# Decode attention plus gated MLP on one core: heads taken in pairs, projections and output sums moved to VectorE, and every engine's program made of loops

## The chip, the cores and the metric

The kernel runs on one core of one Trainium2 chip. The metric is the device time of one execution in microseconds (us). Before the change the median of 3 runs is 745.85 us (745.75 to 746.23). A core has five engines with programs of their own: TensorE (PE, its weight loads shown as PEld), VectorE (DVE), ScalarE (ACT), GpSimd (POOL) and SyncE (SP), which here issues nearly all loads. Programs meet only at semaphores.

## The reference

One token x of 576 elements is normalised; the result goes through attention over a cache of 8192 positions with 32 heads of 128, and through a gated MLP of 4608; both outputs are added to x. All is float32.

```
xn = layernorm(x)
q = (xn @ wq), 32 heads of 128
scores = q . k_cache / sqrt(128);  p = softmax(scores);  o = p . v_cache
A = o.reshape(4096) @ wo
h = relu(xn @ W_gate) * (xn @ W_up)
out = x + A + h @ W_down
```

The inputs are 134.2 MB of keys, as much of values, and 50.8 MB of weights: 319.2 MB read once, with two operations or so per element.

## The kernel before, in words

A *tile* is 128 partitions by 16384 floats, 8.389 MB, and SBUF holds three of them (`slots`). For head n the tile `("t", n)` carries the values of head n-1 (tile 0: weights) beside the keys of head n, so that a slot is free when TensorE has used those values (mark `("V", n-4)`) and VectorE those keys (`("mr", n-3)`). SyncE's program (`load`, line 159, called from lines 164 to 181) is one list of loads on one queue, each with its wait: three weight tiles, 32 key-and-value tiles, the last values with gate weights and nine output chunks, then the other output weights in shrinking pieces, then the output.

Before the heads, TensorE multiplies xn with wq, W_gate and W_up in 512-column pieces (lines 222 to 231 and `gates`); q is turned into a column per head (`turn`, `qs`).

Each key tile has 128 partitions with 64 positions each. For each head VectorE multiplies all 64 x 128 elements by the query, which TensorE has spread over all partitions in PSUM (`product`, line 287), sums them to 64 scores a partition (`sums`, line 292) and takes their maximum mr (line 293). TensorE spreads the 128 maxima over the partitions (`maxima`), VectorE reduces them to a common bound nb (`bound`, line 296), ScalarE makes the exponentials (`soft`, line 306), and TensorE multiplies them with the values (`values`), into bank bo. After three heads (G = 3) ScalarE copies bo out (`rows`, line 310), TensorE folds it (`outputs`), and VectorE divides by the sums (`close`, lines 299 and 300). TensorE's ten turns of three heads are a loop (`repeat`, `emit`); the programs of the other engines are written out in full.

At the end TensorE multiplies each of 68 output chunks of 128 x 576 (32 of wo, 36 of W_down) with its column of os or hh, into two banks, which are added (line 412) and copied out (lines 413 and 414).

Of the kernel before, what the change touches and what calls it, by code (L numbers as in the profile page):

```python
# [3 lines left out]
F32 = mybir.dt.float32  # L4
# [3 lines left out]
PE_ENGINE = mybir.EngineType.PE  # L8
# [9 lines left out]
G = 3  # L18
NIT = (H - 2) // G
# [5 lines left out]
OUT = ((9,), (28,), (9, 7, 5, 4, 3), (1, 1, 1))  # L25

LAST = 4

UNITS = (28, 32, 16, 5)


STEP = 16

HEAD = 12


class Program:
# [4 lines left out]

    def __init__(self, nc):
        self.nc = nc
        self.sems = {}
        self.counts = {}
        self.marks = {}
        self.lists = {e: [] for e in ("sync", "scalar", "vector", "gpsimd", "tensor")}
        self.loop = None

    def sem(self, name):
        if name not in self.sems:
            self.sems[name] = self.nc.alloc_semaphore(f"s_{name}")
            self.counts[name] = 0
        return self.sems[name]

    def add(self, engine, f, waits=(), mark=None, on=None, by=1):
        to = None
        if mark is not None:
            to = on or engine  # L60
            self.sem(to)
            self.counts[to] += by
            assert mark not in self.marks, mark
            self.marks[mark] = (to, self.counts[to])
        self.lists[engine].append((f, tuple(waits), to, by))

    def repeat(self, begin, times, renamed):


        self.loop = (begin, len(self.lists["tensor"]), times)  # L70
        base = sum(to is not None for _, _, to, _ in self.lists["tensor"][:begin])
        body = {m: v for m, (to, v) in self.marks.items() if to == "tensor" and v > base}
        for m in body:
            del self.marks[m]
        for k in range(times):
            for m, v in body.items():
                self.marks[renamed(m, k)] = ("tensor", v + k * len(body))
        self.counts["tensor"] += (times - 1) * len(body)

    def emit(self, engine, eng):  # L80
        lines = self.lists[engine]
        if engine == "tensor":
            begin, end, times = self.loop
            self.run(eng, lines[:begin])
            with self.nc.Fori(STEP, STEP * (times + 1), STEP, engines=[PE_ENGINE], head_slot={PE_ENGINE: HEAD}) as i:
                self.run(eng, lines[begin:end], i)
            self.run(eng, lines[end:])
        else:
            self.run(eng, lines)

    def run(self, eng, lines, counter=None):
        for f, waits, to, by in lines:
            need = {}
            for w in waits:
                if w[0] == "round":
                    eng.wait_ge(self.sem(w[1]), counter)
                    continue
                s, v = self.marks[w]
                need[s] = max(need.get(s, 0), v)
            for s, v in need.items():  # L100
                eng.wait_ge(self.sem(s), v)  # L101
            i = f(eng)
            if to is not None:
                i.then_inc(self.sem(to), by)


def build(nc, x, kv, vw, wq, wqt, wg, wod, out):
    pr = Program(nc)
    add = pr.add

# [6 lines left out]
    slots = [sb(f"slot{i}", [P, W]) for i in range(3)]  # L117
    ident = sb("ident", [P, P])
    sel = sb("sel", [P, 4 * G])
    x2 = sb("x2", [P, N2])  # L120
    ones = sb("ones", [P, 1])
    one = ones[:1, :]
    eps = sb("eps", [1, 1])
    sm = sb("sm", [1, 8])
# [5 lines left out]
    xn = pzs[:1, :6 * P]  # L130
    xz = sb("xz", [P, 4, 37])
    xt = sb("xt", [P, 37])
    row = sb("row", [P, 576])
    xr = row[:1, :]
    row = row[:, :512]
    gr = sb("gr", [P, 512])
    qs = sb("qs", [P, H])
    dq = sb("dq", [P, G, P])
    hh = sb("hh", [P, 4, 9])
    os = sb("os", [P, H])  # L140
# [6 lines left out]
    bq, bb, bm, bo, bt, acc, ac2, bx = [bank(f"bank{i}") for i in range(8)]  # L147
    qb = bb[:, :G * DH].rearrange("p (h d) -> p h d", d=DH)
    pm = bm[:, :P]
    px = bm[:, 128:136]  # L150
    ot = bt[:, :G]
    pl = bt[:, 8:8 + G]
    turned = bx.rearrange("p (b n) -> p b n", b=4)
# [3 lines left out]
    def load(name, k, src, waits, on, start=0):  # L157
        dst = slots[k % 3][:, start:start + src.shape[-1]]
        add("sync", lambda e: e.dma_start(dst, src), waits, name, on=on, by=16)  # L159

    def tile(n):
        return slots[(n + 3) % 3]

    load("wq", 0, wq, (), "dwq")
    load("g0", 1, wqt, (), "dg0")
    load("g1", 2, wg, (), "dg1")
    load(("t", 0), 3, kv[0], ("pq",), "dt0")
    load(("t", 1), 4, kv[1], ("u0",), "land0")
    load(("t", 2), 5, kv[2], ("u1",), "land1")
    load(("t", 3), 6, kv[3], ("u2", ("mr", 0)), "land2")  # L170
    for n in range(4, H):
        load(("t", n), n + 3, kv[n], (("V", n - 4), ("mr", n - 3)), f"land{(n - 1) % G}" if n < H - 1 else "dlast")
    load(("t", H), H + 3, vw, (("V", H - 4), ("mr", H - 3)), "dvw")
    f = OUT[0][0]
    for k, loads in enumerate(OUT[1:]):
        free = ((("V", H - 3), ("mr", H - 2)), (("V", H - 2), ("mr", H - 1)), (("V", H - 1), "u3", ("first", OUT[0][0] - 1)))[k]
        i = 0
        for n in loads:
            load(("o", f), H + 4 + k, wod[:, (f - 9) * D:(f - 9 + n) * D], free, f"do{f}", i * D)
            i += n  # L180
            f += n
    add("sync", lambda e: e.dma_start(out, xr), (("end", 0), ("end", 1)), "out", on="dout", by=16)


    add("gpsimd", lambda e: e.memset(ident, 0.0), (), "id0")
    add("gpsimd", lambda e: e.affine_select(out=ident, in_=ident, compare_op=ALU.not_equal, fill=1.0, base=0,
                                            pattern=[[-1, P]], channel_multiplier=1), ("id0",), "ident")
    add("gpsimd", lambda e: e.memset(x2, 0.0), (), "x20")
    add("gpsimd", lambda e: e.memset(xz, 0.0), (), "xz0")
    add("gpsimd", lambda e: e.memset(xt, 0.0), (), "xt0")  # L190
    add("gpsimd", lambda e: e.memset(pzs, 0.0), ("px",), "pz0")


    add("scalar", lambda e: e.dma_start(xr, x), (), "xr", on="dxr", by=16)
    add("scalar", lambda e: e.dma_start(x2[64:P:32, :], x.rearrange("o (j q) -> (o j) q", j=2)), ("x20",), "x2", on="dx2", by=16)
    add("vector", lambda e: e.memset(ones, 1.0))
    add("vector", lambda e: e.memset(eps, EPS))
    add("vector", lambda e: e.memset(xn, 0.0), (), "n0")
    add("vector", lambda e: e.reduce_sum(sm[:, 0:1], xr, axis=AX.X), ("xr",), "n1")
    add("vector", lambda e: e.tensor_scalar_mul(sm[:, 1:2], sm[:, 0:1], 1.0 / D), ("n1",), "n2")  # L200
    add("vector", lambda e: e.tensor_scalar(xr, xr, sm[:, 1:2], None, op0=ALU.subtract), ("n2",), "n3")
    add("scalar", lambda e: e.activation(xn[:, :D], xr, AF.Square, accum_out=sm[:, 2:3]), ("n3",), "n4")
    add("scalar", lambda e: e.activation(sm[:, 3:4], sm[:, 2:3], AF.Sqrt, bias=eps, scale=1.0 / D), ("n4",), "n5")
    add("vector", lambda e: e.reciprocal(sm[:, 4:5], sm[:, 3:4]), ("n5",), "n6")
    add("vector", lambda e: e.tensor_scalar_mul(xn[:, :D], xr, sm[:, 4:5]), ("n6",), "n7")
    add("vector", lambda e: e.tensor_copy(xn[:, 704:768], xn[:, 512:576]), ("n7",), "xn")

    add("vector", lambda e: e.reduce_sum(sel, ident.rearrange("p (j m) -> p m j", j=4)[:, :4 * G, :], axis=AX.X), ("ident",), "sel")
    for name, t in (("bo", bo), ("acc", acc), ("ac2", ac2)):
        add("vector", lambda e, t=t: e.memset(t, 0.0), (), name + "0")  # L210

    add("vector", lambda e: e.tensor_copy(xz[:, :, 5], px[:, :4]), ("px", "xz0"), "xz")
    add("vector", lambda e: e.tensor_copy(xt[:, 5:7], px[:, 4:6]), ("xt0",), "xt")

    def mm(waits, mark, o, lhsT, rhs, start, stop):
        add("tensor", lambda e: e.matmul(o, lhsT, rhs, start=start, stop=stop), waits, mark)  # L216

    for a in range(6):
        mm(("xn",) if a == 0 else (), "px" if a == 5 else None, px[:, a:a + 1], xn[:, a * P:(a + 1) * P], one, True, True)


    for k in range(36):
        if k < 32:
# [8 lines left out]
    def turn(rows, waits, mark):  # L232
        for b in range(4):
            add("tensor", lambda e, b=b: e.transpose(turned[:, b, :], rows[:, b * P:(b + 1) * P], ident),
                waits if b == 0 else (), mark if b == 3 else None)
# [239 lines left out]
```

## Time and profile before

| what | number |
|---|---|
| median of 3 runs | 745.85 us |
| the profiled execution | 745.72 us |
| its span, first to last instruction | 744.2 us |
| VectorE busy | 577.2 us (78%) |
| TensorE busy | 302.0 us (41%) |
| ScalarE busy | 36.5 us (5%) |
| read from HBM | 319.16 MB, 429 GB/s over the span |

The page divides the span into 40 slices and gives each engine's busy share of a slice in tenths; the DMA row is the mean busy share of the 16 DMA engines. Groups list a kind of instruction with its count, busy time and mean ns of one, and behind the bar the idle time before it and what ended that. The chain follows the last instruction back to what released it. A wait is put down to what came last.

### The profile page before, as it was taken

Reading aid. Unit: us, or ns where it says so; the run is one execution under the profiler, and the core shown is the slowest. Engines: PE = TensorE matmul, PEld = TensorE weight load, DVE = VectorE, ACT = ScalarE, POOL = GpSimd, SP = SyncE. Lnnn points to the kernel's source line nnn. Section 1 sums busy time; section 2 is a strip of 40 time slices with the busy share of each in tenths; the row PEclk is TensorE's granted clock in tenths of the full one; section 3 lists DMA queues with packets and bytes.
Section 4 is the critical chain, followed back from the end, with each engine's and each line's share of the span. In section 5 each row is a group of like instructions: output and inputs, shape, how many; then the busy total and the mean of one; then the engine's idle time right before and its main releaser. Section 6 shows DMA issues by size and latency. Waiting matters only on the chain.

```text
span 744.2 us, 4062 instructions
## 1 busy us (share of the span) xinstructions
PE 302.0 (41%) x1752; PEld 87.4 (12%) x1752; DVE 577.2 (78%) x177; ACT 36.5 (5%) x114; POOL 2.1 (0%) x10
## 2 busy tenths in 40 slices
PE   1454413343253343352343344334324325334677
PEld 1111100010010010010010011001001001001122
DVE  2000189999989999989999998998998998999610
ACT  1000001010010010010000001001001000000000
POOL 1000000000000000000000000000000000000000
PEclk9967755767655565556556656655565565565789
DMA  9999999999999999999999999999999999999997
GB/s 395 451 420 426 445 451 402 440 451 405 444 447 413 444 437 444 416 440 444 412 440 447 412 440 444 412 447 437 437 423 440 444 412 437 451 409 438 432 414 319
DMA packets 6498, 319.30 MB, mean 429 GB/s; under 512 B 724, under 2 KB 726, under 8 KB 1240
## 3 DMA queue, kind: packets, MB, share of 16 engines
q1 hardware_dynamic: 6482, 319.17, 99.3%
q8 instruction: 6, 0.10, 0.1%
q14 instruction: 4, 0.03, 0.0%
q10 hardware_dynamic: 6, 0.00, 0.0%
HBM read 319.16 MB, written 0.00 MB: 429 GB/s over the span
## 4 chain that ended last, share of the span: by engine, by line
DMA 45%; DVE 22%; issue 20%; PE 11%; ACT 1%; SPq 0%; DVEq 0%; ACTq 0%
DMA slot<-in_kv 35%; DVE slot L287 12%; PE bank L216 11%; DVE s L292 9%; DMA slot<-in_wqt 5%; DMA slot<-in_wod 5%; ACT row L310 1%; ACT pzs L306 0%; DVE nb L296 0%; DVE mr L293 0%; SPq L159 0%; DVE os L300 0%; DVE row L413 0%; DVE rl L299 0%; DVEq L101 0%
## 5 line engine op out<-in xcount | busy, mean ns | idle before, releaser
L287 DVE TENSOR_TENSOR slot<-slot,bank 128x8192 f32<-128x8192 f32 x32 | 277.9, 8686 | 82.3 <-PE bank L216 65.8
L292 DVE TENSOR_REDUCE s<-slot 128x64 f32<-128x8192 f32 x32 | 277.6, 8676 | 0.0
L216 PE MATMUL bank<-slot,pzs 128*12 128x512 f32 x1024 | 184.7, 888 | 201.9 <-ACT pzs L306 201.9
L216 PEld LDWEIGHTS bank<-slot,pzs 128*12 128x12 f32 x1024 | 35.4, 123 | 332.5 <-issue 332.3
L216 PE MATMUL bank<-slot,xz 128*32 128x512 f32 x208 | 36.7, 732 | 32.1 <-DMA slot<-in_wq 12.8
L216 PE MATMUL bank<-ident,mr 128*128 128x128 f32 x64 | 17.6, 360 | 73.8 <-DVE mr L293 73.7
L216 PE MATMUL bank<-l,ones 128*128 128x3 f32 (+1 forms) x22 | 6.3, 354 | 98.2 <-ACT pzs L306 98.2
L306 ACT ACTIVATE pzs<-s,nb 128x64 f32<-128x64 f32 x32 | 11.1, 348 | 457.3 <-issue 419.4
L237 DVE TENSOR_SCALAR row<-bank 128x512 f32<-128x512 f32 x1 | 0.7, 692 | 33.8 <-PE bank L216 33.8
L216 PEld LDWEIGHTS bank<-ident,mr 128*128 128x128 f32 x64 | 10.7, 210 | 95.6 <-DVE mr L293 95.4
L412 DVE TENSOR_TENSOR x<-bank,x 64x288 f32<-64x288 f32 x1 | 0.5, 460 | 26.9 <-PE bank L216 26.9
L216 PEld LDWEIGHTS bank<-l,ones 128*128 128x128 f32 x22 | 5.3, 299 | 101.5 <-ACT pzs L306 100.7
L274 ACT ACTIVATE dq<-ident,qs 128x128 f32<-128x128 f32 x32 | 10.7, 392 | 130.7 <-PE bank L216 90.6
L216 PE MATMUL bank<-dq,ones 128*128 128x384 f32 (+1 forms) x24 | 15.3, 737 | 0.0
L216 PEld LDWEIGHTS bank<-slot,xz 128*32 128x32 f32 x208 | 8.5, 131 | 57.8 <-issue 23.6
L216 PE MATMUL bank<-sel,row 128*128 128x3 f32 (+1 forms) x88 | 11.6, 254 | 7.9 <-ACT row L310 7.9
L216 PE MATMUL bank<-slot,os 128*1 128x288 f32 x128 | 11.3, 500 | 4.7 <-DMA slot<-in_wod 4.7
L216 PEld LDWEIGHTS bank<-sel,row 128*128 128x128 f32 x88 | 10.6, 191 | 17.5 <-ACT row L310 17.5
L216 PE MATMUL bank<-slot,hh 128*1 128x288 f32 x144 | 11.2, 406 | 3.2 <-DMA slot<-in_wod 3.2
L216 PE MATMUL bank<-slot,xt 128*32 128x512 f32 x26 | 6.8, 1021 | 10.8 <-DMA slot<-in_wqt 10.8
L310 ACT COPY row<-bank 128x512 f32<-128x512 f32 x11 | 6.4, 585 | 77.2 <-PE bank L216 77.2
L296 DVE TENSOR_REDUCE nb<-bank 128x1 f32<-128x128 f32 x32 | 9.1, 284 | 0.6 <-PE bank L216 0.6
(52 smaller groups left out, 54.3 us busy)
## 6 DMA issues: line engine op xcount, KB each, us to landing
slot<-in_wod SPq DMA_DIRECT2D x1, 8064.0 KB, 39.3
slot<-in_vw SPq DMA_DIRECT2D x1, 7968.0 KB, 39.6
slot<-in_wod SPq DMA_DIRECT2D x1, 2592.0 KB, 25.9
slot<-in_wod SPq DMA_DIRECT2D x1, 2016.0 KB, 30.4
slot<-in_wod SPq DMA_DIRECT2D x1, 1440.0 KB, 33.3
slot<-in_wod SPq DMA_DIRECT2D x1, 1152.0 KB, 35.6
slot<-in_wod SPq DMA_DIRECT2D x1, 864.0 KB, 36.9
slot<-in_wod SPq DMA_DIRECT2D x3, 288.0 KB, 25.0
```

What stands on the lines that cost most here:

```text
L216: add("tensor", lambda e: e.matmul(o, lhsT, rhs, start=start, stop=stop), waits, mark)
L237: add("vector", lambda e: e.tensor_scalar_mul(row, bq, SCALE), ("pq", "n7"), "qr")
L274: add("scalar", lambda e, m=m, h=h: e.activation(dq[:, m, :], ident, AF.Copy, scale=qs[:, h:h + 1]), (free,) if m == 0 else (), ("dq", k) ...
L287: add("vector", lambda e: e.tensor_mul(k3, k3, qb[:, m, None, :].to_broadcast([P, C, DH])), waits, ("mul", h))
L292: add("vector", lambda e: e.reduce_sum(s, k3, axis=AX.X), (("mul", h),), ("sum", h))
L296: add("vector", lambda e: e.tensor_reduce(nb[h % 2], pm, axis=AX.X, op=ALU.max, negate=True), (("pm", h),), ("nb", h))
L306: add("scalar", lambda e: e.activation(pz[:, i, :, 4 * G - 4:4 * G], s2[h % 2].rearrange("p (c b) -> p c b", b=4), AF.Exp, bias=nb[h % 2], ...
L310: add("scalar", lambda e: e.copy(row, bo), (("V", h),) + ((("ot", k - 1),) if k else ("pqt",)), ("oc", k), on="oc", by=STEP)
L412: add("vector", lambda e: e.tensor_add(x2[64:P, :], ac2[64:P, :N2], x2[64:P, :]), ("odd", "x2"), "y")
```

## The change

The kernel is written anew around short programs. In the order of the work:

- **Layout.** Three slots remain, but with fixed roles: two hold the keys of a *pair* of heads each (`KEYS`), one the values of a pair (`VALUES`). G becomes 2, and there are 16 pairs (NP).
- **q, gate, up.** The rows of wq, W_gate and W_up come transposed, as 104 chunks of 128 outputs by 576, in four tiles of 26 chunks (7.668 MB). xn is spread over all partitions, in PSUM (`xp`) and SBUF (`xb`). Each chunk times xn, summed along its row, gives 128 outputs in one column of `dots`. VectorE does this in one fused instruction per chunk (`dot`): all 26 of the first tile, 14 of each other one. The other 12 of a tile GpSimd multiplies in one instruction (`others`) and ScalarE sums one by one (`total`).
- **Queries.** GpSimd makes the diagonals for TensorE's spreading (`diagonals`), which ScalarE did before.
- **Pairs.** VectorE's loop does product, bound of the head before, sums, for both heads, then `close`. TensorE's loop does one pair's values, with the query for a later pair between its two heads. SyncE's loop loads the keys of pair i+2 when VectorE is done with pair i, and the values of pair i+1 when TensorE is done with those of pair i (vb).
- **Output.** 62 of the 68 chunks are added by VectorE into one row of sums per partition (`acc`): a fused multiply by the chunk's column of `coef` and add. 60 of them stand in a loop of 15 rounds, which waits for `chunks`, a count that SyncE raises when enough chunks have landed; two follow. TensorE does the last 6 and adds acc over the partitions.
- **Programs.** VectorE, ScalarE and TensorE run theirs inside a loop of one turn, whose start is put at a given place in a block of instructions (`HEADS`).

The core of the diff, loads and waits first:

```diff
-G = 3
+G = 2
+NP = H // G
+MINE = 14
+LOADS = (27, 5, 4, 4, 4, 4, 4, 4, 4, 2, 2, 2, 1, 1)
+ROUNDS = 15
+LAST = 6
+    KEYS = (slots[:, :W], slots[:, W:2 * W])
+    VALUES = slots[:, 2 * W:]
+    def passed(sem, to, by):
+        add("sync", lambda e: e.sem_inc(pr.sems[to], by), ((sem, 16),))
...
+    load(tile(3), wl[3], (("dots", A),), "dl3")
+    passed("dl2", "wl", 1)
+    load(KEYS[0], kk[0], (("dots", A + B), ("sums", OTHERS)), "dk0")
+    passed("dl3", "wl", 1)
+    load(KEYS[1], kk[1], (("dots", A + 2 * B), ("sums", 2 * OTHERS)), "dk1")
+    passed("dk0", "kland", 16)
+    load(VALUES, vv[0], (("dots", A + 3 * B), ("sums", 3 * OTHERS)), "vland")
+    passed("dk1", "kland", 16)
+    pr.loop("sync", 1, NP - 1)
...
+    add("sync", keys, (("sumb", lambda i: i), ("kland", lambda i: i * 16 + 16)), "kland", 16)
+    add("sync", lambda e, i: e.dma_start(VALUES, vv[ds(i, 1), :, :].rearrange("o p w -> (o p) w")),
+        (("vb", lambda i: i),), "vland", 16)
+    pr.done("sync")
+    for k, n in enumerate(LOADS):
+        if k == 1:
+            load(VALUES, vv[NP - 1], (("vb", NP - 1),), "vland")
+        waits = {0: (("sumb", NP - 1),), 1: (("sumb", NP),), 8: (("vb", NP),)}.get(k, ())
+        load(slots[:, OUT + f * D:][:, :n * D], wod[:, f * D:(f + n) * D], waits, f"do{k}")
...
+    for k in range(max(places[:4 * ROUNDS]) + 1):
+        full = sum(places[4 * m + 3] <= k for m in range(ROUNDS))
+        if full > ready:
+            passed(f"do{k}", "chunks", (full - ready))
+            ready = full
...
+            return e.scalar_tensor_tensor(out=c, in0=c, scalar=1.0, in1=xp, op0=ALU.mult, op1=ALU.mult,
+                                          accum_out=dots[:, ds(column(i), 1)])
...
+    values(0, (("vland", lambda i: i * 16),))
+    query((("dq", lambda i: i), ("mulb", lambda i: i + 1)))
+    values(1, ())
...
+    pr.loop("vector", 1, ROUNDS + 1)
+    for m in range(4):
+        def chunk(e, i, m=m):
+            c = slots[:, ds(i * (4 * D) + (OUT - 4 * D + m * D), D)]
+            return e.scalar_tensor_tensor(out=acc, in0=c, scalar=coef[:, ds(i * 4 + (m - 4), 1)], in1=acc, op0=ALU.mult, op1=ALU.add)
+        waits = ((f"acc{'dabc'[m]}", lambda i: i),) if m else (("chunks", lambda i: i), ("accd", lambda i: i))
+        add("vector", chunk, waits, f"acc{'abcd'[m]}", 1)
+    pr.done("vector")
```

The first place is the end of SyncE's program, the loads behind the last keys. In the kernel before (vw is the last values, wod the output weights, mr and vector VectorE's marks, tensor TensorE's):

```order
L159 DMA slot<-in_kv 128x16384 [waits s_mr0,s_tensor]
L159 DMA slot<-in_vw 128x15936 [waits s_mr1,s_tensor]
L159 DMA slot<-in_wod 128x16128 [waits s_mr2,s_tensor]
L159 DMA slot<-in_wod 128x5184 [waits s_vector,s_tensor]
L159 DMA slot<-in_wod 128x4032 [waits s_vector,s_tensor]
L159 DMA slot<-in_wod 128x2880 [waits s_vector,s_tensor]
L159 DMA slot<-in_wod 128x2304 [waits s_vector,s_tensor]
L159 DMA slot<-in_wod 128x1728 [waits s_vector,s_tensor]
L159 DMA slot<-in_wod 128x576 [waits s_tensor] x3
L182 DMA out_y<-row 1x576 [waits s_scalar,s_vector]
```

In the changed kernel (sumb: VectorE's second sums of a round; vb: TensorE's second values of a round; do0 to do13: the landings of the output loads; waits that only raise a count are shown with the next row):

```order
L154 DMA slots<-in_wod 128x15552 [waits s_sumb]
L154 DMA slots<-in_vv 128x16384 [waits s_vb]
L154 DMA slots<-in_wod 128x2880 [waits s_sumb]
L154 DMA slots<-in_wod 128x2304 x6
L154 DMA slots<-in_wod 128x2304 [waits s_vb]
L154 DMA slots<-in_wod 128x1152 x3
L154 DMA slots<-in_wod 128x576 x2
L200 DMA out_y<-xb 1x576 [waits s_do0,s_do1,s_do2,s_do3,s_do4,s_do5,s_do6,s_do7,s_do8,s_end1,s_end0]
```

Output loads now stand on both sides of the last values, and the waits for do0 to do8, after each of which SyncE raises `chunks`, stand behind all the issues, the one that waits for vb among them.

The second place is SyncE's loop over the pairs in the changed kernel, where before stood one load a head:

```order
L94 ISA [waits s_sumb]
L180 ISA [waits s_kland]
L180 REGISTER_ALU
L180 ISA
L180 DMA slots<-in_kk 128x16384
L182 ISA [waits s_vb]
L182 DMA slots<-in_vv 128x16384
L87 REGISTER_ALU
L87 COMPARE_AND_BRANCH
```

A load of keys now waits for VectorE alone and a load of values for TensorE alone, one behind the other in the same program.

The third place is the end of VectorE's program. Before, what follows the last head:

```order
L356 TENSOR_TENSOR hh<-hh,bank 128x4 [waits s_vector]
L357 TENSOR_TENSOR hh<-hh,bank 128x4 [waits s_vector]
L299 RECIPROCAL rl<-bank 128x2 [waits s_tensor]
L300 TENSOR_TENSOR os<-bank,rl 128x2 [waits s_vector]
L412 TENSOR_TENSOR x<-bank,x 64x288 [waits s_dx2,s_tensor]
L413 COPY row<-bank 1x288 [waits s_tensor]
```

In the changed kernel, from the last product for the MLP on (the loop of four chunks, then close and the two chunks behind it; acca to accd are marks of VectorE's own chunks):

```order
L323 TENSOR_TENSOR coef<-coef,dots 128x36 [waits s_mra]
L87 UNCONDITIONAL_BRANCH
L380 ISA [waits s_accd,s_chunks]
L380 ISA
L380 SCALAR_TENSOR_TENSOR acc<-slots,coef,acc 128x576
L380 ISA [waits s_acca]
L380 SCALAR_TENSOR_TENSOR acc<-slots,coef,acc 128x576
L380 ISA [waits s_accb]
...
L388 SCALAR_TENSOR_TENSOR acc<-slots,coef,acc 128x576 [waits s_accd,s_do9]
L388 SCALAR_TENSOR_TENSOR acc<-slots,coef,acc 128x576 [waits s_acce]
L401 COPY xb<-bank 1x288 [waits s_even]
```

The sum over the output chunks, which was TensorE's, now stands at the end of VectorE's program, each chunk behind the one before.

More of the change, by code (lines that the diff above doesn't have):

```diff
@@ L45, in __init__ @@
         self.sems = {}
[L46 to L49, printed above, removed]
+        self.lists = {e: [] for e in ENGINES}
     def sem(self, name):
@@ L67, in repeat @@
[L67 to L87, printed above, removed]
-        else:
[L89 to L104, printed above, removed]
@@ L173, in build @@
[L173 to L182, printed above, removed]
@@ L309, in rows, with load, tile @@
-    def rows(k, h):
-        add("scalar", lambda e: e.copy(row, bo), (("V", h),) + ((("ot", k - 1),) if k else ("pqt",)), ("oc", k), on="oc", by=STEP)
-    def values(i, t, waits, mark, end):
+    def load(dst, src, waits, to):
+        add("sync", lambda e: e.dma_start(dst, src), waits, to, 16)
+    def passed(sem, to, by):
+        add("sync", lambda e: e.sem_inc(pr.sems[to], by), ((sem, 16),))
+        pr.sem(to)
+    def tile(k):
+        return slots[:, (k + 2) % 3 * W:][:, :PER * D]
+    for k in range(3):
+        load(tile(k), wl[k], (), f"dl{k}")
```

491 lines of the change are left out of this document (234 added, 257 removed).

## The prediction

> **What bounds the kernel now.** I read the page's head, slices, and queue table first, then the windows, chain and timeline.
>
> ```profile
> span 744.2 us, 4062 instructions
> DVE  2000189999989999989999998998998998999610
> DMA  9999999999999999999999999999999999999997
> q1 hardware_dynamic: 6482, 319.17, 99.3%
> ```
>
> The one load queue has packets under way for 99.3% of the span; VectorE is dense too, but has gaps. Windows over the first tile's wait and over one turn of three heads (core's time, PE, PEld, DVE, ACT, POOL, then clock, DMA share, GB/s) show the stream's pace:
>
> ```profile
> 22.50:41.80 19.30, 8.53 (x64) 2.12 (x64) 0.00 (x0) 0.00 (x0) 0.00 (x0) 0.84 1.00 435
> 390.12:448.15 58.03, 21.55 (x116) 6.18 (x115) 53.36 (x14) 2.89 (x10) 0.00 (x0) 0.62 1.00 434
> ```
>
> Three tiles of 8.389 MB in 58.03 us is 19.35 us each, with the queue's share at 1.00; VectorE works 53.36 of the 58.03, or 17.8 per head, so it has 1.6 us to spare per head. The transfers set the time. Before the first landing the stream has a start and an end of its own:
>
> ```profile
> 0.74 0.40 SPq L159 DMA_DIRECT2D slot<-in_wq  x1
> 1.20 0.42 SPq L159 DMA_DIRECT2D slot<-in_wqt  x1
> 1.66 0.42 SPq L159 DMA_DIRECT2D slot<-in_wg  x1
> 22.53 3.81 PE L216 MATMUL bank<-slot,xz 128*32 128x512 f32 x20 [12.77 <-DMA slot<-in_wq]
> ```
>
> The tile issued at 0.74 releases TensorE at 22.53: 19.35 plus 2.44 us that a stream on an empty queue pays. SyncE issues loads 0.46 apart. At the other end:
>
> ```profile
> 740.83 0.66 PE L216 MATMUL bank<-x,ident 128*1 128x288 f32 x4
> 742.50 0.45 DVE L413 COPY row<-bank 1x288 f32<-1x288 f32 x1 [1.93 <-PE bank L216]
> 742.97 0.32 SPq L182 DMA_DIRECT2D out_y<-row  x1
> ```
>
> From the last correction product (740.83) to the copy is 1.67, from the copy to the end 1.70. The profiled execution took 745.72, so 1.52 lies outside its span; the median is 745.85, and I take the sum as good for both.
>
> **The change, part by part.** The bytes are the same 319.16 MB, so the stream still needs some 735 us at 434 GB/s if it never stops. Fewer instructions buy nothing by themselves where the queue is full. What decides is whether the new buffers keep the queue fed and what is left after its last byte. I follow the landings.
>
> *Weights.* Four tiles of 7.668 MB, 17.69 each, land at 20.9, 38.6, 56.2 and 73.9, if the fourth is issued in time. VectorE makes 26 fused products-and-sums of 576 from the first tile, then 14 a tile; GpSimd multiplies the other 12 in one instruction, ScalarE sums them. None of the three stands in the trace; nearest are:
>
> ```profile
> L237 DVE TENSOR_SCALAR row<-bank 128x512 f32<-128x512 f32 x1 | 0.7, 692 | 33.8 <-PE bank L216 33.8
> L412 DVE TENSOR_TENSOR x<-bank,x 64x288 f32<-64x288 f32 x1 | 0.5, 460 | 26.9 <-PE bank L216 26.9
> L191 POOL MEMSET pzs<- 128x960 f32 x1 | 0.9, 897 | 7.9 <-PE bank L216 7.9
> L202 ACT ACTIVATE pzs<-row 1x576 f32<-1x576 f32 x1 | 0.7, 682 | 0.0
> L202 ACT ACTIVATION_READ_ACCUMULATOR pzs<-row 1x1 f32 x1 | 0.2, 185 | 0.0
> ```
>
> By the first two rows 224 elements more cost 232 ns, so 576 cost 0.76; I take 0.95 for a dot with its sum and loop (0.76 to twice that, as the sum is unseen). VectorE ends the tiles at 45.6, 58.9, 72.2 and 87.2. The fourth tile needs the first free (45.6, long before the queue empties at 56.2). The first keys need tile two free: GpSimd from 38.6, then twelve sums at 0.87 plus some loop, 12 us; this hides as long as GpSimd takes under 73.9-38.6-12 = 23 us. By the memset's rate 6912 elements are 6.5 us, three times that still 19. So nothing is lost here, and the cover is that queue; each us of GpSimd above 23 would show in the end time. The removed TensorE weights work and its turn through row and PSUM also lay under the stream: zero.
>
> *First pairs.* Keys K1 and K2, values V1, then keys K3, land at 93.3, 112.6, 132.0 and 151.3. A round on VectorE, from the chain:
>
> ```profile
> 221.73 8.69 DVE slot L287
> 230.42 0.20 DVE nb L296
> 230.62 0.10 DVE rl L299
> ...
> 230.74 0.16 DVE os L300
> 230.91 8.60 DVE s L292
> ...
> 239.60 0.22 DVE mr L293
> 239.82 8.60 DVE slot L287
> ```
>
> Two heads make 2 x (8.69 + 0.20 + 8.60 + 0.22) + 0.26 = 35.6. Round 1 starts with K1 at 93.3, round 2 at 128.9. There is one buffer of values, so V2 is issued (line 182, waiting for vb) only when TensorE has used V1; and TensorE's loop puts the next query, which waits for VectorE's second product of round 2 (mulb, line 366), between the two heads' values. That product ends at 128.9 + 26.3 = 155.2. TensorE's pieces:
>
> ```profile
> 324.16 6.15 PE L216 MATMUL bank<-slot,pzs 128*12 128x512 f32 x32
> 332.04 0.49 PE L216 MATMUL bank<-ident,mr 128*128 128x128 f32 x2
> 332.49 1.45 PE L216 MATMUL bank<-dq,ones 128*128 128x384 f32 x2
> ```
>
> A query of 256 columns is 1.0, a head's values 6.15: V1 is free at 162.4, while K3 had landed at 151.3 with nothing behind it. V2 lands at 162.4 + 2.44 + 19.35 = 184.2 instead of 170.7: **13.5 us lost**, and the stream doesn't win them back. I keep 8 (values faster) to 18 (slower dots delay K1). From there each round is 38.7 against VectorE's 35.6: values are free 33.5 after a round's keys land, 5 before the queue runs out. No further stop.
>
> *The end.* K4 lands at 203.5, K16 at 203.5 + 12 x 38.7 = 667.9, V15 at 687.3, the first 27 output chunks (7.963 MB, 18.4) at 705.6, V16 at 725.0. VectorE's round 16 is over at 703.5. Its 60 looped chunks (lines 376 to 383) wait for counts that SyncE adds (line 198). These stand in SyncE's program behind *all* issues, and one of these, load 8 (line 189), waits until TensorE has used V16: 725.0 + 6.15 + 1.0 + 6.15 = 738.3. Six issues at 0.46 follow, so counts come at 741.1. VectorE is idle from 704 to 741 with 27 chunks landed. The transfers themselves end near 752; then the chunk sum is the bound. Each adds into the same acc and waits for the one before, as here:
>
> ```profile
> 711.59 0.19 DVE L355 TENSOR_SCALAR hh<-bank 128x32 f32<-128x32 f32 x1 [3.76 <-PE bank L234]
> 711.82 0.19 DVE L356 TENSOR_TENSOR hh<-hh,bank 128x32 f32<-128x32 f32 x1
> ```
>
> Such a wait adds 0.04. With 0.76 that is 0.80, the lower bound if register work and the coefficient by pointer hide; a SyncE issue, the dearest sequencer step shown (0.4), on top of each makes 1.20, the upper. I take 0.95, near the row: 60 x 0.95 = 57.0, to 798.1. [...] Then close and two chunks 2.2, the correction and last products 2.5 (1.67 at full clock, longer on an idle TensorE), copy and output 1.7: 804.5, and 1.52 outside: **806 us**.
>
> **The rivals.**
>
> *Counts in time* (0.05): if they came as chunks land, the sum would start at 705.6, end at 762.6, in all 806 - 35.5 = 770.5. The order of SyncE speaks against it.
>
> *No stop for V2* (0.05): 806 - 13.5 = 792.5. One buffer and mulb speak against it.
>
> *A fused operation that runs two passes* (0.07): 1.52 a pass, so some 1.6 a dot and 1.71 a chunk. Round 1 starts at 129.7 instead of 93.3 (+36), the 62 chunks cost 47 more: 889. The trace has no fused operation with a sum to exclude it.
>
> *Loops that reload their code* (0.05). The row that bears on it is TensorE's present loop: its return lies between the products at 332.04 and 332.49, which only the 0.49 of the first separates. [...] Its price as a mechanism here: a small transfer beside the big ones,
>
> ```profile
> 0.73 0.52 ACTq L194 DMA_DIRECT2D row<-in_x  x1
> 2.07 0.74 DVE L199 TENSOR_REDUCE sm<-row 1x1 f32<-1x576 f32 x1 [0.36 <-DMA row<-in_x]
> ```
>
> 1.34 us. 34 returns of the dot loops put round 1 at 131 (+38), fifteen of the chunk loop add 20: 864.
>
> *A faster stream* (0.06), the one on the other side: whole-key and whole-value transfers could move quicker. The stop and the tail cost 60 over before; the 307.1 MB up to V16 take 707.5 at 434 GB/s and would have to take 647, so it decides at 474 GB/s; at 480 the time is 806 - 68 = 738. The windows' 434 and 435 at share 1.00 speak against it.
>
> **How the numbers follow.** 0.72 stays for the forecast, 806. Its bounds: the chunk price moves it by -9 to +15, the stop by -5.5 to +4.5, GpSimd or the clock by some us. The range is 786 to 830: it holds the forecast and the missing stop; left out are counts in time, two passes, reloads and the faster stream, 0.23 in all less what smaller forms of them keep inside. A measurement of this kernel tells about 0.2% from no change. Slower: 0.72 + 0.05 + 0.05 + 0.07 + 0.05 = 0.94. Of the faster stream's 0.06 I give 0.05 to faster and 0.01 to landing within 0.2%.
>
> **What would show it.** Right: the first slices of the queue full, one slice near 151 to 165 us with a hole, then full again; VectorE idle for some 37 us near the end, released by SyncE right after TensorE's last values; then about sixty operations of line 380, near 0.95 apart, while the queue's slices fall to nothing. Wrong: the chunk operations beginning when the first 27 chunks land; dots at 1.5 or more; a gap before each first operation of a loop's turn; or a rate above 440 GB/s in the middle windows.

## The result, and the profile after

| | before | after |
|---|---|---|
| median | 746.04 us (4 runs, 745.75 to 747.55) | 810.7 us (4 runs, 808.81 to 811.49) |
| ratio | | 1.086 (95% interval 1.083 to 1.088) |
| the profiled execution | 745.72 us | 811.15 us |
| its span | 744.2 us | 809.4 us |

The change makes the kernel 8.6% slower. Here are the head, VectorE's and the DMA's slices and the load queue from the page of the changed kernel:

```profile
span 809.4 us, 4277 instructions
DVE  1855599999999898989898989898989898903776
DMA  9999999489999999999999999999999999999300
q1 hardware_dynamic: 7202, 319.17, 91.5%
```

The bytes are the same, but the queue now has packets under way for 91.5% of the span, where it had 99.3%. The DMA row has two defects: one slice at 4 (142 to 162 us), and the last three at 3, 0 and 0. In VectorE's row the slice at 0 (708 to 728 us) and the dense ones behind it belong to the second defect. The windows of the changed kernel (columns as in the prediction) price them: a stretch of one pair in the middle, then the first defect, then three stretches at the end.

```profile
283.10:321.80 38.70, 12.99 (x80) 4.50 (x80) 35.72 (x10) 1.47 (x5) 0.61 (x1) 0.63 1.00 434
...
150.50:166.00 15.50, 11.41 (x74) 3.03 (x66) 15.46 (x3) 1.03 (x3) 0.62 (x1) 0.89 0.20 68
...
707.90:740.78 32.88, 12.90 (x79) 3.88 (x79) 0.00 (x0) 0.59 (x1) 0.00 (x0) 0.62 0.97 414
740.78:752.50 11.72, 0.00 (x0) 0.00 (x0) 9.42 (x12) 0.00 (x0) 0.00 (x0) 0.60 1.01 418
752.50:802.57 50.07, 4.01 (x16) 0.87 (x16) 39.60 (x49) 0.00 (x0) 0.00 (x0) 0.53 0.05 19
```

A pair takes 38.70 us at share 1.00 and 434 GB/s, as before. Around 158 us the queue is nearly empty for 15.5 us (share 0.20, 68 GB/s). From 707.90 to 740.78 VectorE does nothing while the transfers run on; behind 752.5 the transfers are over, and VectorE adds for 50 us more. The timeline shows who held the queue at the first defect, SyncE's issues first (start, duration, engine and line, operation), then TensorE's work:

```profile
130.71 0.36 SPq L180 DMA_DIRECT2D slots<-in_kk  x1
164.22 0.36 SPq L182 DMA_DIRECT2D slots<-in_vv  x1
167.34 0.35 SPq L180 DMA_DIRECT2D slots<-in_kk  x1
```

```profile
149.42 0.79 PE L231 MATMUL bank<-ident,mr 128*128 128x128 f32 x2 [7.78 <-DVE mr L298]
150.14 4.79 PE L231 MATMUL bank<-slots,pzs 128*8 128x512 f32 x32
158.11 0.67 PE L231 MATMUL bank<-dq,ones 128*128 128x256 f32 x2 [3.17 <-DVE slots L289]
158.71 5.32 PE L231 MATMUL bank<-slots,pzs 128*8 128x512 f32 x32
```

Between two issues of SyncE lie 33.5 us, and the second comes when TensorE has done with V1's second head. TensorE had stood 3.17 us on the query, which waited for VectorE's product, between the two heads; and ahead of the first head's values it had already stood 7.78 us on the maxima of the next pair, which wait for VectorE too. At the end of the kernel VectorE's rows read:

```profile
740.78 0.82 DVE L380 SCALAR_TENSOR_TENSOR acc<-slots,coef,acc 128x576 f32<-128x576 f32 x1 [32.88 <-SPq L157]
741.79 0.82 DVE L380 SCALAR_TENSOR_TENSOR acc<-slots,coef,acc 128x576 f32<-128x576 f32 x1 [0.19 <-DVE acc L380]
...
744.94 0.82 DVE L380 SCALAR_TENSOR_TENSOR acc<-slots,coef,acc 128x576 f32<-128x576 f32 x1 [0.33 <-DVE acc L380]
```

The first of the 60 adds waits 32.88 us for SyncE's count. Then an add follows the last one after 1.00 us, and after 1.15 at a return of the loop: the 60 of them last until 802.57, 1.03 each. Of the 65.2 us between the two spans, some 15 belong to the empty queue and some 50 to the adds.

### The profile page after: what moved, and what is told of

Read it like the earlier page. It is cut to its first block, busy times and chain, and to the rows that moved or that the text cites. A ratio compares the mean times of both kernels' runs of the same rounds, so it can differ in the third digit from the quotient of the medians.

```text
span 809.4 us, 4277 instructions
## 1 busy us (share of the span) xinstructions
PE 221.1 (27%) x1320; PEld 76.4 (9%) x1320; DVE 674.0 (83%) x377; ACT 56.9 (7%) x161; POOL 56.2 (7%) x29
## 3 DMA queue, kind: packets, MB, share of 16 engines
q1 hardware_dynamic: 7202, 319.17, 91.5%
## 4 chain that ended last, share of the span: by engine, by line
DMA 70%; DVE 19%; issue 4%; PE 3%; POOL 2%; DVEq 1%; ACTq 1%; SPq 1%; ACT 0%; POOLq 0%
DMA slots<-in_kk 65%; DVE slots L289 6%; DVE acc L380 6%; DVE s L296 5%; DMA slots<-in_vv 3%; PE bank L231 2%; POOL slots L221 2%; DMA xr<-in_x 1%; DVEq L380 1%; ACTq L281 0%; SPq L154 0%; PE xp L231 0%; SPq L180 0%; ACT slots L281 0%; DVE acc L388 0%
## 5 line engine op out<-in xcount | busy, mean ns | idle before, releaser
L289 DVE TENSOR_TENSOR slots<-slots,bank 128x8192 f32 x32 | 277.9, 8685 | 44.6 <-DMA slots<-in_kk 33.7
L296 DVE TENSOR_REDUCE s<-slots 128x64 f32 x32 | 277.6, 8674 | 0.0
L231 PE MATMUL bank<-slots,pzs 128*8 128x512 f32 x1024 | 147.2, 727 | 23.2 <-DMA slots<-in_vv 23.2
L380 DVE SCALAR_TENSOR_TENSOR acc<-slots,coef,acc 128x576 f32<-128x576 f32 x60 | 49.1, 818 | 45.7 <-SPq L157 32.9
L259 DVE SCALAR_TENSOR_TENSOR slots<-slots,xp 128x576 f32 x68 | 46.2, 749 | 18.5 <-SPq L157 18.2
L221 POOL TENSOR_TENSOR slots<-slots,xb 128x6912 f32<-128x6912 f32 x3 | 44.4, 14808 | 40.2 <-SPq L157 40.2
L231 PEld LDWEIGHTS bank<-slots,pzs 128*8 128x8 f32 x1024 | 27.8, 102 | 122.5 <-issue 95.2
L231 PE MATMUL bank<-dq,ones 128*128 128x256 f32 x36 | 13.1, 449 | 81.4 <-POOL dq L214 41.0
L281 ACT ACTIVATE slots<-slots x36 | 24.6, 683 | 53.7 <-POOL slots L221 53.7
L231 PE MATMUL bank<-sel,row 128*128 128x2 f32 x128 | 16.9, 254 | 11.3 <-ACT row L338 11.3
L231 PEld LDWEIGHTS bank<-sel,row 128*128 128x128 f32 x128 | 15.5, 191 | 26.1 <-ACT row L338 26.1
## 6 DMA issues: line engine op xcount, KB each, us to landing
slots<-in_wod SPq DMA_DIRECT2D x2, 288.0 KB, 15.5
```

Source lines behind the costliest of these rows:

```text
L221: return e.tensor_mul(c, c, xb[:, None, :].to_broadcast([P, OTHERS, D]))
L231: add("tensor", lambda e, *i: e.matmul(o, lhsT, rhs, start=start, stop=stop), waits, to, by)
L259: return e.scalar_tensor_tensor(out=c, in0=c, scalar=1.0, in1=xp, op0=ALU.mult, op1=ALU.mult, accum_out=dots[:, ds(column(i), 1)])
L281: return e.activation(c, c, AF.Copy, accum_out=dots[:, ds(within(t * MINE + i + (PER + MINE), PER + MINE, DOTS - 1), 1)])
L289: return e.tensor_mul(k3, k3, qb[:, m, None, :].to_broadcast([P, C, DH]))
L296: return e.reduce_sum(s2[m], k3, axis=AX.X)
```

## The experiments

The theory: two mechanisms make the loss, the stop of the queue at the second pair's values and the late, serial adds at the end. The rivals are named with each run. All of these kernels compute the whole result; ratios are to the kernel before on the same chip, with 95% intervals.

**The counts moved ahead of the load that waits.** SyncE raises `chunks` for the first four output loads before it issues load 8, which waits for TensorE's last values. The rest is unchanged.

```diff
     for k, n in enumerate(LOADS):
+        if k == 8:
+            for early in range(4):
+                count(early)
```

> SyncE raises the counts for the first four output loads before it waits for the last values' release, instead of after all issues. Late start (theory): VectorE's sixty adds begin near 708, where its last product for the MLP ended in the changed kernel's trace, instead of at 740.8, and go on at 1.04 each; the end moves by the 33 us that VectorE idled, to 778 us (775 to 781). Rival, that adds cannot run beside the transfers (they wait for landings, or the writes of the loads slow them): the adds begin early but stretch to 1.5 or more each while loads land, and the time falls by under 15 us, to 796 or more.

Measured: 778.1 us (777.92 to 779.66), ratio 1.043 (1.041 to 1.044). The timeline shows the first add (the loop's line is 388 here) and the windows how the adds go beside transfers:

```profile
709.29 0.82 DVE L388 SCALAR_TENSOR_TENSOR acc<-slots,coef,acc 128x576 f32<-128x576 f32 x1 [1.22 <-SPq L157]
```

```profile
709.29:740.00 30.71, 11.39 (x76) 3.25 (x76) 24.41 (x30) 0.59 (x1) 0.00 (x0) 0.64 0.96 411
```

The adds start 31.5 us earlier, and the time falls by 32.6. With the queue at 0.96 there are 30 adds in 30.71 us, 1.02 each: they do not slow down beside transfers. So the place of the counts in SyncE's program held VectorE, nothing else.

**Two sums in turn.** Even chunks are added into `acc`, odd ones into `xb` (zeroed before), so that no add needs the one right before it and each waits for the last but one; TensorE sums both at the end.

```diff
+        t = (acc, xb)[m % 2]
-            return e.scalar_tensor_tensor(out=acc, in0=c, scalar=coef[...], in1=acc, ...)
+            return e.scalar_tensor_tensor(out=t, in0=c, scalar=coef[...], in1=t, ...)
```

> The adds alternate between two rows of sums, so that each waits for the add before the last one; the counts stay late. If the 0.18 between adds is the wait for the one just before and the register work behind it (theory), it lies under the running add: spacing falls from 1.04 to about 0.75 and the time by 17 us, to 794 (788 to 798). Rival, that the 0.18 to 0.33 is the sequencer's own time for each add whatever it waits for: spacing stays above 0.95, the time above 805.

Measured: 794.1 us (792.32 to 795.19), ratio 1.064 (1.062 to 1.066). The first adds in its timeline (line 383 here):

```profile
740.76 0.82 DVE L383 SCALAR_TENSOR_TENSOR acc<-slots,coef,acc 128x576 f32<-128x576 f32 x1 [32.22 <-SPq L157]
741.49 0.81 DVE L383 SCALAR_TENSOR_TENSOR xb<-slots,coef,xb 128x576 f32<-128x576 f32 x1
```

The adds start at the same time as in the changed kernel, but lie 0.73 apart, the return of the loop included. So 0.27 of each 1.00 was the wait for the add before, and 60 x 0.27 = 16.2 is nearly the 16.6 gained.

**Most adds given back to TensorE.** VectorE's loop does 24 chunks, two follow it, and TensorE does 42.

```diff
-ROUNDS = 15
-LAST = 6
+ROUNDS = 6
+LAST = 42
```

> VectorE keeps 26 of the output chunks, TensorE does 42; the counts stay late. Theory: VectorE still starts near 740.8, 24 adds at 1.04 and two more end near 767.5, TensorE's 40 chunks lie beside them, and the time is 774 us (770 to 778). Rival, that the late start is owed to TensorE's values and TensorE then becomes the bound: its 42 chunks at 0.4 begin after 740 with the landings and end later than VectorE's, 780 or more.

Measured: 771.8 us (771.67 to 772.24), ratio 1.035 (1.033 to 1.036). TensorE's chunks in its timeline:

```profile
737.55 19.57 PE L231 MATMUL bank<-slots,coef 128*1 128x288 f32 x160
765.14 1.13 PE L231 MATMUL bank<-acc,ones 128*1 128x288 f32 x4 [8.02 <-DVE acc L388]
```

TensorE takes 40 chunks in 19.57 us, 0.49 each against VectorE's 1.03, and then still waits 8.02 us for the end of VectorE's 26. The size of VectorE's share, not the change of engine at the end, sets the time.

**The values in two halves.** V of each pair is loaded as two transfers, one a head, each when TensorE is done with that head; TensorE still waits for both before a pair.

```diff
-    add("sync", lambda e, i: e.dma_start(VALUES, ...),
-        (("vb", lambda i: i),), "vland", 16)
+    add("sync", lambda e, i: e.dma_start(VALUES[:, :SK], ...),
+        (("va", lambda i: i),), "vland", 16)
+    add("sync", lambda e, i: e.dma_start(VALUES[:, SK:], ...),
+        (("vb", lambda i: i),), "vlandb", 16)
```

> The values of a pair come in two loads of one head each; the first half is issued when TensorE has used the first head's values. Theory, that the hole from 150.5 to 166 comes from the one values buffer being released as a whole: the first half is issued near 155, 8 us earlier, and flows for 9.7 us while the second half is released; the hole shrinks to about 7 and the time to 802.5 us (800 to 805). Rival, that the hole comes from VectorE's late release of keys (the third keys are issued at 130.7): nothing moves, 810 to 811.

Measured: 804.2 us (803.73 to 805.16), ratio 1.078 (1.076 to 1.080). SyncE's issues and the windows at the stop:

```profile
156.62 0.36 SPq L183 DMA_DIRECT2D slots<-in_vv  x1
162.58 0.34 SPq L185 DMA_DIRECT2D slots<-in_vv  x1
```

```profile
150.50:158.00 7.50, 5.92 (x32) 0.94 (x24) 7.50 (x1) 0.00 (x0) 0.00 (x0) 1.00 0.24 66
158.00:166.00 8.00, 5.28 (x42) 2.04 (x42) 7.97 (x3) 1.03 (x3) 0.61 (x1) 0.98 0.92 397
```

The first half goes 7.6 us earlier than V2 did, the stop ends at 158 instead of 166, and the time falls by 6.5. The single buffer is a part of the cause.

**Counts early and adds on TensorE together.** The first and the third edit.

> Early counts and TensorE's 42 chunks together. Theory: VectorE's 26 adds run from 709 to 736 under the transfers, nothing of the sum is left behind the last byte, and the end is bound by the load stream again, with its hole: last landing near 752, 4 to 5 us of last products, copy and store, 757 to 759 us. Rival, that the sum on two engines beside the stream costs it speed or TensorE falls behind the landings: 763 or more.

Measured: 762.4 us (761.83 to 763.96), ratio 1.022 (1.020 to 1.024): above the 757 to 759 of the theory, just under the 763 of the rival. Its TensorE in the timeline:

```profile
737.90 19.57 PE L239 MATMUL bank<-slots,coef 128*1 128x288 f32 x160
757.29 0.66 PE L239 MATMUL bank<-acc,ones 128*1 128x288 f32 x4
```

The theory took TensorE to be done when the last bytes landed. But it comes to the chunks only at 737.90, behind its last values, and 160 products later it is at 757.3, some 4 us after the transfers ended (the queue's share falls to 0.71 from 752 to 754 us). So TensorE fell behind the landings, as the rival said: 42 chunks are too many for it.

**TensorE's first turn in another order.** The first pair is written out ahead of the loop, with both heads' values ahead of the next maxima and the query.

```diff
+    values(0, (("vland", 16),) + ((("vlandb", 16),) if "vlandb" in pr.sems else ()))
+    values(1, ())
+    maxima(0, 2)
+    query((("dq", 1), ("mulb", 2)))
...
+    pr.loop("tensor", 2, NP + 1)
```

> Only TensorE's first turn is written out with another order: the first pair's values before the maxima of the second pair's first head and before the next query; the loop then does turns 2 to 16. Theory: the hole has its length from TensorE's order in that one turn (values wait for the maxima at 149.4 and, for the second head, for the product at 158); the values now run from 141.6, V2 is issued near 153 instead of 164.2, the hole shrinks from 15.5 to 5, the time to 800 us (798 to 802). Rival, that VectorE, which then gets its bound later, falls behind and the hole moves to the next pair: 807 or more.

Measured: 806.5 us (806.29 to 809.28), ratio 1.082 (1.080 to 1.084): 4.2 off, where the theory gave some 10. SyncE's issues and one window, some 37 us behind the stop of the changed kernel:

```profile
151.14 0.36 SPq L182 DMA_DIRECT2D slots<-in_vv  x1
...
199.10 0.34 SPq L182 DMA_DIRECT2D slots<-in_vv  x1
```

```profile
192.00:198.00 6.00, 3.61 (x34) 1.07 (x34) 5.96 (x3) 0.44 (x2) 0.61 (x1) 1.00 0.01 3
```

V2 goes 13 us earlier, but V3's load goes at 199.10, as it did in the changed kernel (199.15), and now no transfer lies ahead of it: the stop has moved by one pair, as the rival had it. The rival's reason was not seen: VectorE starts the third pair at 168.08, and at 168.13 in the changed kernel, so it did not fall behind. So the cause is not the first turn alone.

**Counts early, adds on TensorE, halves and the first turn's order, all together.** No new code.

> Early counts, TensorE's 42 chunks, values in halves, and the first turn in the other order. Theory: the tail and the hole are all that the change costs; without both the stream runs from the first byte to the last but for a short stop at 131 where the third keys are issued late, and the time is 743 us (741 to 746), level with the kernel before or up to 0.5% under it. Rival, that there is a third cost (slower pace with halves, the start with the dots): 749 or more.

Measured: 754.5 us (753.88 to 754.68), ratio 1.011 (1.009 to 1.013), where the theory gave 743, which was wrong; the rival's 749 or more came true. The window shows the moved stop here too:

```profile
186.00:192.00 6.00, 5.68 (x34) 1.40 (x34) 6.00 (x2) 0.00 (x0) 0.00 (x0) 0.70 0.53 229
```

To it comes TensorE's tail, as in the run with counts early and adds on TensorE: its last 8 products start at 750.06, while the queue's share is 0.04 from 746 to 748 us.

**The same, with the keys in halves too**, each half loaded when VectorE has summed that head.

```diff
+    for m in range(2):
+        add("sync", keys, (("sum" + "ab"[m], lambda i: i), (land, lambda i: i * 16 + 16)), land, 16)
```

> As the one before, and the keys in halves too, each issued when VectorE has summed the head whose place it takes. Theory: the stop at 131 is the third keys' wait for the whole first pair; with halves it goes, 0.8 to 1.5 us less than the kernel without it, 742 us. Rival, that the stop is the restart of the queue after the weights, whatever the keys wait for: same time as the one before within 0.3 us.

Measured: 756.4 us (755.45 to 756.87), ratio 1.014 (1.012 to 1.016): no gain, but 1.9 more. The later stop is the same as in the run before (a share of 0.57 from 186 to 192 us, where it had 0.53). Theory and rival both looked at a stop near 131 us, but there is none to take away: from 126 to 138 us the share is 1.00 or more in both runs. Most of the 1.9 lies in the transfers. The queue's row of this page:

```profile
q1 hardware_dynamic: 11522, 319.17, 98.6%
```

The same bytes go in 11522 packets instead of 9506, and packets are under way for 98.6% of 753.7, 743.1 us, instead of 98.5% of 752.9, 741.6. Why more packets should take longer no run shows.

**Values first in every turn.** Halves as above, each waited for by its own head's values, and the order within TensorE's loop changed; counts and adds as in the changed kernel. The lines are shown against the run with the values in halves.

```diff
-    maxima(0, lambda i: i + 1)
-    values(0, (("vland", lambda i: i * 16), ("vlandb", lambda i: i * 16)))
-    query((("dq", lambda i: i), ("mulb", lambda i: i + 1)))
-    values(1, ())
+    values(0, (("vland", lambda i: i * 16),))
+    values(1, (("vlandb", lambda i: i * 16),))
+    maxima(0, lambda i: i + 1)
+    query((("dq", lambda i: i), ("mulb", lambda i: i + 1)))
```

> The changed kernel with values in halves, each half waited for by itself, and in every turn TensorE does both heads' values before the maxima of the next pair's first head and before the query. Counts stay late, VectorE keeps its 62 chunks. Theory (from the kernel with the other order in its first turn alone, whose hole moved to 192 to 199): the hole is VectorE's late start, 36.6 a round against two key tiles that landed 19.4 apart, and TensorE's order makes the values' release wait for VectorE's next round; if the release hangs on TensorE alone in every turn, VectorE wins its 2 us a round back without a stop, the hole goes and the time is 796 us (794 to 798). Rival, that VectorE then waits in every round for the maxima behind the values: rounds of 40 or more in the second half, 810 or more.

Measured: 795.7 us (795.48 to 796.73), ratio 1.067 (1.065 to 1.068), 15.0 below the changed kernel. The DMA row of its page, and SyncE's issues:

```profile
DMA  9999999999999999999999999999999999999300
```

```profile
148.55 0.36 SPq L183 DMA_DIRECT2D slots<-in_vv  x1
151.99 0.34 SPq L185 DMA_DIRECT2D slots<-in_vv  x1
...
183.94 0.35 SPq L183 DMA_DIRECT2D slots<-in_vv  x1
187.37 0.34 SPq L185 DMA_DIRECT2D slots<-in_vv  x1
```

V2 and V3 are both asked for 12 to 16 us before the changed kernel asked, and no slice is low any more ahead of the adds. This is the whole of the first defect: 15.0 us, of which the halves alone gave 6.5.

**All mended.** Values first, halves, counts early, and the adds divided as 38 for VectorE and 30 for TensorE (ROUNDS 9, LAST 30).

> As the one before, with early counts, and the output sum split 38 chunks to VectorE, 30 to TensorE (with 42 TensorE ended 4.6 us behind the last landing, at 0.485 a chunk). Theory: hole and tail are then both gone, the last landing is near 738, 743.5 us (742 to 746), level with the kernel before or some 0.3% under it: what the change cost was these two and nothing else. Rival, that a third cost of 5 us or more is left (rounds of VectorE over the stream's 38.7, the start with the dots): 749 or more.

Measured: 748.9 us (748.26 to 749.37), ratio 1.0037 (1.0023 to 1.0050), 5 above the theory and just under the 749 of the rival, a third cost. The head, the DMA row, the load queue and TensorE's last chunks:

```profile
span 746.5 us, 4430 instructions
DMA  9999999999999999999999999999999999999997
q1 hardware_dynamic: 9506, 319.17, 99.3%
```

```profile
742.19 1.14 PE L243 MATMUL bank<-slots,coef 128*1 128x288 f32 x8 [0.24 <-DMA slots<-in_wod]
```

Both defects are gone, and TensorE's last products wait for the last bytes. Of the 3.0 us that remain, the two spans show 2.3, and most of these are no stop: the queue's share is 99.3% in both kernels, and 99.3% of 746.5 is 741.3 us, of 744.2 it is 739.0. The same bytes were under way for 2.3 us more, in 9506 packets instead of 6482. That the smaller transfers of the halves cost this pace is likely, by the run with key halves, but not shown: no run changes the packets alone. So the kernel comes within 0.4% of the kernel before, and none of these versions beats it.

**More on GpSimd.** As the changed kernel, but GpSimd takes 18 of 26 chunks of a tile instead of 12 (MINE 8 instead of 14), which takes away the cover that its work had under the weight tiles.

```diff
-MINE = 14
+MINE = 8
```

> The changed kernel with 8 instead of 14 dots of each later weight tile on VectorE, so 18 for GpSimd (22.2 us by its 14.8 for 12) and ScalarE (13.7). The first keys are then issued at 76 instead of 64, behind the empty queue, and land near 98 instead of 94.4; the second keys are issued near 99.5 and land near 121, the first values near 143: three stops of the stream of some 11 us in all. Theory, that the hole behind the third keys is set by VectorE, which starts with the first keys, so that stops ahead of it are taken out of the hole: the time rises only by the 3.5 us that the first keys are later, to 814 us (812.5 to 816). Rival, that the stream's stops add up: 11 us more, 820 or above. No change in time would say that the weights phase has more cover than the trace shows.

Measured: 816.0 us (815.56 to 818.01), ratio 1.095 (1.093 to 1.096): 5.3 over the changed kernel, and within the theory's 812.5 to 816. Two windows of the changed kernel, then the same of this one:

```profile
60.00:150.00 90.00, 3.96 (x10) 2.51 (x10) 71.20 (x67) 24.68 (x65) 27.81 (x3) 1.00 1.01 435
150.00:200.00 50.00, 23.82 (x150) 6.97 (x150) 49.06 (x13) 2.50 (x8) 1.23 (x2) 0.73 0.73 312
```

```profile
60.00:150.00 90.00, 4.59 (x10) 2.50 (x10) 56.58 (x41) 43.27 (x113) 47.93 (x6) 1.00 0.89 376
150.00:200.00 50.00, 18.77 (x114) 5.89 (x114) 49.06 (x13) 1.47 (x5) 0.61 (x1) 0.76 0.86 364
```

The queue stops for 90 x (1.01 - 0.89) = 10.8 us more ahead of the first pairs, and for 50 x (0.86 - 0.73) = 6.5 less behind. The difference, 4.3, is near the 5.3 measured. So these stops do not add up. SyncE's timeline shows what counts:

```profile
169.21 0.36 SPq L182 DMA_DIRECT2D slots<-in_vv  x1
```

V2's load, which ends the later stop, is issued at 169.21 instead of 164.22. The early stops cost these 5.0 us; the rest of them only takes the place of the later one.

## Why the prediction was right, point by point

The forecast was 806 us, and 810.7 was measured. The two mechanisms were the ones named, at the places named.

*The stream* held its pace: 434 GB/s in the middle, transfers over at 752.5 where the sum had "near 752". No row bears out the rival of a faster stream.

*The weights* lay under the stream, as said. Groups of the changed kernel give what the trace before could only bound:

```profile
L380 DVE SCALAR_TENSOR_TENSOR acc<-slots,coef,acc 128x576 f32<-128x576 f32 x60 | 49.1, 818 | 45.7 <-SPq L157 32.9
L259 DVE SCALAR_TENSOR_TENSOR slots<-slots,xp 128x576 f32 x68 | 46.2, 749 | 18.5 <-SPq L157 18.2
...
L221 POOL TENSOR_TENSOR slots<-slots,xb 128x6912 f32<-128x6912 f32 x3 | 44.4, 14808 | 40.2 <-SPq L157 40.2
```

A dot takes 0.749, about its lower bound of 0.76 and not the 0.95 taken; GpSimd's multiply takes 14.8, between 6.5 and 19 and inside the cover of 23. The prediction said that each us beyond that cover would show in the end time. The run with more on GpSimd corrects this: with GpSimd at 22.1 and 18 sums behind it, 10.8 us of new stops show as some 5, because the rest falls together with the later stop. The rival of two passes falls with the first two rows.

*The stop for V2* was put at 151 to 162.4 with V2's buffer and the product in the way; the issue came at 164.22. Two terms inside it were off, and in part cancel. Round 2 of VectorE started at 131.51 instead of 128.9, since round 1 started at 94.86 and not at 93.3, and a pair takes 36.65 and not 35.6 (the prediction's own pieces add up to 35.7):

```profile
131.51 8.69 DVE L289 TENSOR_TENSOR slots<-slots,bank 128x8192 f32 x1 [0.61 <-issue]
...
205.61 8.69 DVE L289 TENSOR_TENSOR slots<-slots,bank 128x8192 f32 x1 [1.45 <-DMA slots<-in_kk]
```

Against that the second head's query and values took 0.67 and 5.32 (rows above) instead of 1.0 and 6.15. The stop's price was 13.5, and the run with values first shows 15.0. What the prediction had too narrow is the cause. It named one buffer and the query between the heads, left out the maxima ahead of the first head's values (the 7.78 us above), and took all this as special to the second pair. The run with another first turn shows that the stop is carried by VectorE's lag: K1 and K2 lie in the queue one right behind the other, 19.35 apart, while VectorE needs 36.65 for a pair, and it wins back only 38.70 - 36.65 = 2.05 a turn. Until then every turn of TensorE that puts a wait for VectorE ahead of values frees the buffer late. In the changed kernel "no further stop" came true because the first stop itself took the lag away: the row at 205.61 shows VectorE waiting 1.45 for keys again, in round 4.

*The counts* were forecast for 741.1 and came at 740.78. That they came so near is in part luck: in TensorE's timeline the last values begin at 727.00, 2.0 later than forecast, and with the query between the heads they take 10.7 us instead of 13.3. The run with early counts shows the mechanism alone, worth 32.6 against the 35.5 of its rival, which had the adds start at 705.6. They started at 709.29: VectorE was done at 708.1 and then waited 1.22 for the count.

*The chunks* are the mis-sized term: 60 x 0.95 = 57.0 was forecast, 61.8 measured, and this 4.8 is about all of the miss of 4.7. The step that was off is "such a wait adds 0.04", from a row of two small operations, which made 0.80 the lower bound and 0.95 the price. Here the add itself takes 0.82, and between an add and the one that needs it lie 0.18, and 0.33 at a return. The run with two sums shows it from the other side: 0.73 apart without that wait. A return of the loop adds 0.15 to the spacing, 1.15 against 1.00. What the sum's 2.5 for the correction and last products adds to the row's 1.67, "longer on an idle TensorE", was the author's estimate. These 12 products, up to the copy, took 3.09 here (804.59 to 807.68, behind 47.76 us without work, at a granted clock of 0.51) and 1.68 in the run with counts early and adds on TensorE (757.29 to 758.97, right behind other products).

*Loops that reload their code* is refuted where they were most feared: a return costs VectorE 0.15 in the adds, and 0.61 stands ahead of round 2, a return with its address work; the 68 dots have 18.5 us of idle time ahead of them, of which 18.2 are waits for SyncE, so their 34 returns cost 0.3 at most. That rival's price of 1.34 each was the author's estimate, the time of one small load; that a return has to load code at all, no run shows. The queue tables of the two profiles show how little code was to be saved by short programs, here before, then after:

```profile
q8 instruction: 6, 0.10, 0.1%
q14 instruction: 4, 0.03, 0.0%
```

```profile
q14 instruction: 2, 0.02, 0.0%
q8 instruction: 1, 0.02, 0.0%
```

Ten packets of code became three, 0.1% of the queues' time: beside a load queue at 99.3% that was worth nothing measurable. With both defects mended the time is 0.4% above the kernel before, so the short programs gave nothing that the runs could show.

Not tried: a weight tile between K1 and K2 in the queue, which would take VectorE's lag away at its root, and a start with fewer weights ahead of the first keys.

## What to carry to other kernels

In this kernel, whose load queue was full for 99.3% of the span before, shorter programs gave nothing, and what counted was what keeps the queue full to the last byte. In such a kernel look for each load's wait, and for what stands *ahead* of it in its issuer's program and in the program of the engine that frees its buffer. A count that tells an engine of landed data must not stand behind an issue that waits for something else, which cost 32.6 us here (counts early). And work that has to follow the last bytes should be short, or divided over engines: a sum into one accumulator cost, with each operation, the wait for the last one, here 0.27 of 1.00 us.

## What the runs showed of the hardware that was not expected

- A fused multiply-and-add of 128 x 576 that needs the result of the one before starts 1.00 us after it, and 0.73 after it if it does not (two sums in turn): less than its own 0.81, so in the trace neighbours overlap. The dependent ones kept their pace, 1.02 each, beside a queue at a share of 0.96 (counts early).
- GpSimd multiplies 128 x 6912 in 14.8 us and 128 x 10368 in 22.1, 2.1 ns per element of a partition in both, beside VectorE's dots.
- A small load issued just behind a big one came late: in the changed kernel x (2.2 KB) is issued by ScalarE at 1.26, half a us behind the first of SyncE's loads, and TensorE can use it only at 11.9 us; before, it was issued at 0.73, beside the first of them, and VectorE had it at 2.07. That the big loads hold it up is not shown on its own.

```profile
11.90 2.39 PE L231 MATMUL xp<-xr,ones 1*128 1x512 f32 x4 [11.90 <-DMA xr<-in_x]
```

The normalisation was done at 20.3, 2 us ahead of the first tile's first dot at 22.36, so this cost nothing, but by little.
